# A late operand load moved behind the last transposed rows, and six result stores cut in two, in a fused backward kernel

## The chip, the cores and the metric

The kernel runs on one core of a Trainium2 chip. The metric is the device time of one execution in microseconds (us). Before the change three runs gave 823.28, 824.08 and 824.58 us, a median of 824.08 us.

The core's engines are written as the profile writes them. PE is the matrix engine, PEld is its weight load, DVE is the vector engine, ACT the scalar engine, POOL the general-purpose engine. SP is a sequencer without arithmetic; here it issues most DMAs. ACT and POOL can issue DMAs as well.

## The reference

The reference computes a transformer block and all its gradients, in bfloat16, for 2048 tokens of width 640:

```
h   = x + attn(layernorm(x))          # linear attention, 32 heads
out = h + swiglu(layernorm(h))        # hidden width F = 1728
swiglu(u) = (silu(u @ w1) * (u @ w3)) @ w2
return out, and the gradients of x, wqkv, wo, w1, w3, w2 for a given grad_out
```

The last part of the kernel matters here: the gradients of w1 and w3, each 640 x 1728. They are hn^T @ gg, where hn (2048 x 640) is the normalised input of the MLP and gg (2048 x 3456) holds the gradients behind w1 and w3 side by side. Just before it stands the gradient of x: per 128 tokens, [g_q, g_k, pk] (128 x 1920) times the transposed wqkv.

## The kernel before

The kernel is one hand-ordered program: each engine gets its instructions in the order of the Python code, and waits on semaphores where data must be there first. Two stages concern us.

**The gradient of x** (loop at L1515) runs over t = 0 to 15, 128 tokens each. `e_gxn(t)` (L1495) makes 30 matmuls on PE: two column halves of 320, each of 15 terms. Terms 0 to 4 read the transposed g_q of these tokens, terms 5 to 9 the transposed g_k, terms 10 to 14 `pkT`. The two transposes are DMAs made by `e_T` (L1489 to L1493) and issued by SP three steps ahead: `e_T(t + 3)` stands behind `e_gxn(t)`. They land in one of three buffers in turn, two of them inside `bd`, one named `gT`. After the matmuls, ACT and DVE finish the layer norm's gradient (L1139 to L1152), and SP stores the row (L1522). Every third step also has a small matmul job for another gradient, whose result SP stores at L1337.

**The gradients of w1 and w3** (loop at L1538) run over seven blocks of 496 columns of gg (480 in the last), and in each over m = 0 to 4, 128 rows of the result. One job (`grad_halves`, L1325) is 16 matmuls at L1331 that contract over the tokens. ACT copies the result out of PSUM (L1335) and issues the store (L1337). Eight PSUM buffers are at hand for the jobs (`njob = 8`). The very last job is cut into 352 and 128 columns. A block's operand `gb`, [token, column], is brought in by a transposing DMA from DRAM (`load_block`, L1471 to L1477), with two buffers. Block i + 2 is loaded when block i is through.

Block 0 is loaded in three parts, of 160, 160 and 176 columns, during the stage before: behind the steps t = 7, 9 and 11 (L1525). Block 1 is loaded behind t = 13. All these DMAs are issued by SP, in the order of the code, so a load stands in one queue with the transposes of `e_T` and the stores of L1522.

**Semaphores.** DMAs issued by SP and ACT tell of their landing on eight semaphores, handed out in turn in the order of the code; here they are called 0 to 7. At the end of the program SP waits for each of the eight, 0 first and 7 last, one instruction each, and then the engines meet in a barrier. Before the change the last store of all (128 columns) has semaphore 1, and the one before it (352 columns) has semaphore 0.

```
        if t in (7, 9, 11):
            load_block(0, (t - 7) // 2 * NB0, (t - 5) // 2 * NB0 if t < 11 else NB)
        if t == 13:
            load_block(1)
...
            for a, b in ((0, n - P), (n - P, n)) if last else ((0, n),):
                grad_job(hnN, m, lambda t: gb[i][:, t, a:b], b - a, both_grads(m, f0 + a, f0 + b), A.dma_start)
        load_block(i + 2)
```

Of the kernel before, what the change touches and what calls it, by code (L numbers as in the profile page):

```python
# [20 lines left out]
ST, DT = S // P, D // P  # L21
# [5 lines left out]
NB = 496  # L27
# [28 lines left out]
def kernel(  # L56
# [19 lines left out]
    V, A, T, G, SY = nc.vector, nc.scalar, nc.tensor, nc.gpsimd, nc.sync  # L76
# [901 lines left out]
    for c in range(SC):  # L978
# [9 lines left out]
        for fc in range(FT):  # L988
# [8 lines left out]
            if c == 0 and fc in (5, 7, 9, 11):  # L997
                a, b = {5: (0, 3), 7: (3, 6), 9: (6, 10), 11: (10, 13)}[fc]
# [13 lines left out]
            if c == SC - 1 and fc in (1, 2, 5, 6):  # L1012
                i = (1, 2, 5, 6).index(fc)
# [61 lines left out]
    for fc in range(FT - 1):  # L1075
        b, i = divmod(fc, 4)
# [154 lines left out]
    xnT, pkb, gb = {}, {}, {}  # L1231
# [55 lines left out]
    a, b = ST - 1, ST - 2  # L1287
# [33 lines left out]
    def grad_job(lhs, m, rhs, n, out, q=dma):  # L1321
        for _ in grad_halves(lhs, m, rhs, n, out, q):
            pass

    def grad_halves(lhs, m, rhs, n, out, q=dma):  # L1325

        acc = ps.tile([P, 512], F32, name="job", bufs=njob)
        for t in range(ST):
            if t == ST // 2:
                yield  # L1330
            T.matmul(acc[:, 0:n], lhsT=lhs[:, t, m * P:(m + 1) * P], rhs=rhs(t), start=(t == 0),  # L1331
                     stop=(t == ST - 1))
        ob = obs[:, cnt[0] % (OB // n) * n:(cnt[0] % (OB // n) + 1) * n]
        cnt[0] += 1
        A.copy(out=ob, in_=acc[:, 0:n])  # L1335
        for x, y, to in out:
            q(out=to, in_=ob[:, x:y])  # L1337
# [35 lines left out]
    def fill(n):  # L1373
        for _ in range(n):
            next(jobs, None)
# [55 lines left out]
    for t in range(ST):  # L1431
        c, i = divmod(t, TPC)
# [34 lines left out]
    hnN = bv.tile([P, ST, D], BF16, name="hnN")  # L1467
    blocks = [(f0, min(f0 + NB, 2 * F)) for f0 in range(0, 2 * F, NB)]
    NB0 = 160

    def load_block(i, a=0, b=NB):  # L1471
        if i < len(blocks):
            f0, f1 = blocks[i]
            if a == 0:
                gb[i] = ex.tile([P, ST, NB], BF16, name="gb", bufs=2)
            b = min(b, f1 - f0)
            dmaT(out=gb[i][:, :, a:b], in_=gg_d[f0 + a:f0 + b, :])  # L1477

    def both_grads(m, f0, f1):

        return [(max(f0, lo) - f0, min(f1, lo + F) - f0, out[:, m, max(f0, lo) - lo:min(f1, lo + F) - lo])
                for lo, out in ((0, out4S), (F, out5S)) if max(f0, lo) < min(f1, lo + F)]

    def load_hnN(i):
        dma(out=hnN[:, i * TPC:(i + 1) * TPC, :], in_=hn_v[:, i * TPC:(i + 1) * TPC, :])
# [3 lines left out]
    def e_T(t, k):  # L1489
        if k == 0:  # L1490
            gT[t] = (ex.tile([P, 2 * DT, P], BF16, name="gT") if t % 3 == 2 else
                     bd[:, 2 * (t % 3):2 * (t % 3) + 2, :].rearrange("p c (k q) -> p (c k) q", q=P))
        dmaT(out=gT[t][:, k * DT:(k + 1) * DT, :], in_=gqkv[k][:, t, :])  # L1493

    def e_gxn(t):  # L1495
        acc = ps.tile([P, 2, 512], F32, name="gxn", tag="gxn", bufs=2)
        for j in range(2):
            for k in range(15):
                g = gT[t][:, k, :] if k < 2 * DT else pkT[:, k - 2 * DT, t * P:(t + 1) * P]
                T.matmul(acc[:, j, 0:HD], lhsT=g, rhs=wqT[:, k, j * HD:(j + 1) * HD], start=(k == 0),  # L1500
                         stop=(k == 14))
        gx = scr[:, t % 2, :]
        ln_bwd(acc, t, xnN[:, t, :], ln1, gx, g_h[:, t, :], ex, scr[:, 2 + t % 2, :], scr[:, 4, :])()
        return gx
# [10 lines left out]
    for t in range(ST):  # L1515
        if t > 1 and t % 3 == 0:
            fill(2)
        gx = e_gxn(t)
        if t + 3 < ST:
            for k in range(2):  # L1520
                e_T(t + 3, k)
        dma(out=out1S[:, t, :], in_=gx)  # L1522
        if t in (2, 3, 5, 6):
            load_hnN((2, 3, 5, 6).index(t))
        if t in (7, 9, 11):  # L1525
            load_block(0, (t - 7) // 2 * NB0, (t - 5) // 2 * NB0 if t < 11 else NB)
        if t == 13:
            load_block(1)
    for _ in jobs:
# [8 lines left out]
    for i, (f0, f1) in enumerate(blocks):  # L1538
        n = f1 - f0
        for m in range(DT):  # L1540
            last = (i, m) == (len(blocks) - 1, DT - 1)
            for a, b in ((0, n - P), (n - P, n)) if last else ((0, n),):
                grad_job(hnN, m, lambda t: gb[i][:, t, a:b], b - a, both_grads(m, f0 + a, f0 + b), A.dma_start)
        load_block(i + 2)
    ps.release()
    ex.release()
# [34 lines left out]
```

## Time and profile before

| | |
|---|---|
| runs, us | 823.28, 824.08, 824.58 (median 824.08) |
| the profiled execution, us | 824.66, of which the span in the profile is 822.9 |
| granted clock of PE | 1.0 over the whole span |
| busy: PE, PEld, DVE, ACT, POOL | 99%, 62%, 55%, 40%, 16% |
| stage "gradient of x", us from the span's start | 627 to 702.7 |
| stage "gradients of w1 and w3" | 702.7 to the end |

The span starts with the first instruction and ends with the last. The profile's views that are used are: the page (busy time by engine, the chain of waits that ended last), the list of waits (who waited for whom), the timeline of one engine (start, length, what), the time from issue to landing of a DMA, and the table of busy time and DMA traffic by short windows. A line number names the line of the kernel that made the instruction.

### The profile page before, as it was taken

Reading aid. Unit: us, or ns where it says so; the run is one execution under the profiler, and the core shown is the slowest. Engines: PE = TensorE matmul, PEld = TensorE weight load, DVE = VectorE, ACT = ScalarE, POOL = GpSimd, SP = SyncE. Lnnn points to the kernel's source line nnn. Section 1 sums busy time; section 2 is a strip of 40 time slices with the busy share of each in tenths; the row PEclk is TensorE's granted clock in tenths of the full one; section 3 lists DMA queues with packets and bytes.
Section 4 is the critical chain, followed back from the end, with each engine's and each line's share of the span. In section 5 each row is a group of like instructions: output and inputs, shape, how many; then the busy total and the mean of one; then the engine's idle time right before and its main releaser. Section 6 shows DMA issues by size and latency. Waiting matters only on the chain.

```text
span 822.9 us, 14052 instructions
## 1 busy us (share of the span) xinstructions
PE 814.6 (99%) x5464; PEld 513.2 (62%) x5464; DVE 453.2 (55%) x976; ACT 325.1 (40%) x605; POOL 131.1 (16%) x193
## 2 busy tenths in 40 slices
PE   8999999999999999999999999999999999999998
PEld 5677544555555555777777777777777776544444
DVE  7859887999898576300057777772771545100000
ACT  7856788655565666011112212222212433211111
POOL 2233333323222212100001111110210000000000
PEclk9999999999999999999999999999999999999999
DMA  9999989696475556999878898369997898978661
GB/s 218 260 281 230 209 234 316 194 240 156 145 214 155 171 172 167 241 251 227 241 176 184 215 185 198 58 126 179 234 206 136 169 193 162 223 157 197 166 134 37
DMA packets 321826, 157.57 MB, mean 191 GB/s; under 512 B 240096, under 2 KB 315008, under 8 KB 321760
## 3 DMA queue, kind: packets, MB, share of 16 engines
q1 hardware_dynamic: 279712, 115.85, 62.9%
q10 hardware_dynamic: 34720, 16.34, 9.3%
q0 software_dynamic: 7328, 24.48, 9.2%
q8 instruction: 43, 0.70, 0.4%
q14 instruction: 23, 0.19, 0.1%
HBM read 47.09 MB, written 51.13 MB: 119 GB/s over the span
## 4 chain that ended last, share of the span: by engine, by line
PE 96%; DMA 2%; ACT 1%; SPq 0%; DVE 0%; issue 0%; DVEq 0%; ACTq 0%
PE mm L387 20%; PE job L1331 19%; PE ghn L1127 14%; PE gxn L1500 8%; PE gw L1082 7%; PE o L895 4%; PE big L267 4%; PE o L841 3%; PE gwo L1215 3%; PE gr L1184 3%; PE dkv L1437 3%; PE macc L422 2%; PE at L648 2%; PE mm L267 1%; DMA pqT<-pql 1%; DMA x_sb<-in_A_x_dram 1%
## 5 line engine op out<-in xcount | busy, mean ns | idle before, releaser
L1331 PE MATMUL job<-gb,hnN 128*128 128x496 bf16 (+3 forms) x576 | 116.8, 366 | 0.0
L1127 PEld LDWEIGHTS <-ggb 128*128 128x128 bf16 x864 | 84.5, 98 | 32.8
L1331 PEld LDWEIGHTS <-hnN 128*128 128x128 bf16 x576 | 55.8, 98 | 61.0
L387 PE MATMUL mm<-pqT,w 128*128 128x512 bf16 x405 | 93.6, 379 | 0.0
L387 PEld LDWEIGHTS <-w 128*128 128x128 bf16 x540 | 52.5, 98 | 63.1 <-issue 0.8
L1335 ACT CAST obs<-job 128x496 bf16<-128x496 f32 (+4 forms) x56 | 28.5, 509 | 123.7 <-PE job L1331 123.7
L1127 PE MATMUL ghn<-w13a,ggb 128*128 128x320 bf16 x448 | 63.5, 299 | 0.0
L1142 DVE SCALAR_TENSOR_TENSOR wb<-gs,hnb 128x640 f32<-128x640 bf16 x16 | 13.2, 825 | 89.8 <-ACT gs L1139 89.8
L1127 PE MATMUL ghn<-w13b,ggb 128*128 128x320 bf16 x416 | 61.4, 299 | 0.0
L387 PE MATMUL mm<-g2T,w2T 128*128 128x512 bf16 x240 | 59.6, 379 | 0.0
L1082 PE MATMUL gw<-g,hb 128*128 128x320 bf16 x416 | 56.8, 299 | 0.0
L1192 POOL TENSOR_TENSOR sz<-Zb,g_h 128x640 f32<-128x640 bf16 x16 | 20.2, 1261 | 197.7 <-DVE g_h L1193 197.7
L1082 PEld LDWEIGHTS <-hb 128*128 128x128 bf16 x416 | 40.6, 98 | 16.0 <-issue 0.3
L412 ACT CAST ghh<-mm 128x512 bf16<-128x512 f32 x48 | 28.3, 589 | 45.0 <-PE mm L387 39.7
L778 ACT ACTIVATE sig<-mm 128x512 bf16<-128x512 f32 x56 | 33.7, 602 | 25.6 <-PE mm L387 22.0
L1139 ACT ACTIVATE gs<-ghn 128x640 bf16<-128x640 f32 x16 | 11.2, 703 | 78.8 <-PE ghn L1127 63.2
L387 PEld LDWEIGHTS <-w2T 128*128 128x128 bf16 x260 | 25.3, 98 | 23.5 <-DMA w2T<-in_B_w_dram 0.2
L267 PEld LDWEIGHTS <-pqT 128*128 128x128 bf16 x320 | 30.6, 98 | 14.3 <-issue 1.7
L267 PE MATMUL big<-wqkv,pqT 128*128 128x320 bf16 x250 | 38.5, 299 | 0.3
L1331 PEld LDWEIGHTS <-g 128*128 128x128 bf16 x320 | 31.0, 98 | 11.5
L814 DVE TENSOR_TENSOR gate<-gate,sig 128x1024 bf16<-128x1024 bf16 x28 | 19.3, 689 | 33.5 <-ACT gate L789 33.5
L1500 PE MATMUL gxn<-wqT,bd 128*128 128x320 bf16 x220 | 33.7, 299 | 1.5 <-DMA bd<-g_q 1.1
(216 smaller groups left out, 1373.5 us busy)
## 6 DMA issues: line engine op xcount, KB each, us to landing
hh_d<-hhT SPq DMA_DIRECT2D x24, 256.0 KB, 2.6
gg_d<-gate POOLq DMA_DIRECT2D x24, 256.0 KB, 4.5
gg_d<-ghh POOLq DMA_DIRECT2D x24, 256.0 KB, 3.7
ggb<-gg_d SPq DMA_DIRECT2D x6, 896.0 KB, 5.3
ggb<-gg_d ACTq DMA_DIRECT2D x6, 832.0 KB, 5.8
x_sb<-in_A_x_dram SPq DMA_DIRECT2D x6, 640.0 KB, 5.9
ggb<-gg_d SPq DMA_DIRECT2D x2, 1728.0 KB, 12.9
out_dram<-obs ACTq DMA_DIRECT2D x25, 124.0 KB, 3.1
```

Source lines behind the costliest of these rows:

```text
L267: T.matmul(acc, lhsT=pqT[:, c, t * P:(t + 1) * P], rhs=wqkv[:, c, n0:n0 + HD], start=(c == 0), stop=(c == DT - 1))
L387: T.matmul(acc[:], lhsT=w[:, c, fc * P:(fc + 1) * P], rhs=rhs[:, c, :], start=(c == 0), stop=(c == DT - 1))
L412: A.copy(out=ghh[n // 2][:, n % 2, :], in_=acc[:])
L778: A.activation(sig[:, i, :], gp[:], AF.Sigmoid)
L841: T.matmul(accs[i, j][:, 0:HD], lhsT=hhT[c][:, fc, i * P:(i + 1) * P], rhs=w2[:, fc, j * HD:(j + 1) * HD], start=(first and fc == 0), stop ...
L895: T.matmul(o2["ps"][:, 0:HD], lhsT=hhT[c][:, fc, i * P:(i + 1) * P], rhs=w2[:, fc, j * HD:(j + 1) * HD], start=(fc == 0), stop=(fc == FT - 1))
L1082: T.matmul(acc[:, j, 0:HD], lhsT=hb[b][:, t, i * P:(i + 1) * P], rhs=g2[:, t, j * HD:(j + 1) * HD], start=(t == 0), stop=(t == ST - 1))
L1127: T.matmul(acc[:, j, 0:HD], lhsT=ggb[t // 2][:, k, lo:lo + P], rhs=rhs[:, j * HD:(j + 1) * HD], start=(k == 0), stop=(k == NG - 1))
L1184: T.matmul(gr[t][:, j, 0:HD], lhsT=ghT[t][:, c, :], rhs=wT2[:, c, j * HD:(j + 1) * HD], start=(c == 0), stop=(c == DT - 1))
L1331: T.matmul(acc[:, 0:n], lhsT=lhs[:, t, m * P:(m + 1) * P], rhs=rhs(t), start=(t == 0), stop=(t == ST - 1))
L1335: A.copy(out=ob, in_=acc[:, 0:n])
L1500: T.matmul(acc[:, j, 0:HD], lhsT=g, rhs=wqT[:, k, j * HD:(j + 1) * HD], start=(k == 0), stop=(k == 14))
```

## The change

Two edits. The third part of block 0 (176 columns) is loaded behind step t = 12 and no longer behind t = 11. And the results of the first six jobs of the last stage are stored in two column halves each, 248 columns, where one store of 496 columns was.

```diff
-        if t in (7, 9, 11):
-            load_block(0, (t - 7) // 2 * NB0, (t - 5) // 2 * NB0 if t < 11 else NB)
+        if t in (7, 9, 12):
+            load_block(0, (t - 7) // 2 * NB0, (t - 5) // 2 * NB0 if t < 12 else NB)
...
+                c = (a + b) // 2
+                halves = ((a, c), (c, b)) if i * DT + m < 6 else ((a, b),)
+                out = [(x + y - a, z + y - a, to) for y, w in halves for x, z, to in both_grads(m, f0 + y, f0 + w)]
-                grad_job(hnN, m, lambda t: gb[i][:, t, a:b], b - a, both_grads(m, f0 + a, f0 + b), A.dma_start)
+                grad_job(hnN, m, lambda t: gb[i][:, t, a:b], b - a, out, A.dma_start)
```

The order of SP's DMAs around the first edit (the number in brackets is the step of the row):

```
before: store row (11), LOAD 176, store of a small job, transpose g_q (15), transpose g_k (15),
        store row (12), store row (13), load block 1, store rows (14), (15)
after:  store row (11), store of a small job, transpose g_q (15), transpose g_k (15),
        store row (12), LOAD 176, store row (13), load block 1, store rows (14), (15)
```

The six DMAs that the second edit adds shift the count of semaphores: the last store gets semaphore 7, the one before it semaphore 6. PE, DVE and POOL have the same instructions in the same order as before; ACT has six more DMA issues.

## Prediction

> **What bounds the kernel now.** I read the page first: which engine is busy, and the chain of work that ended last.
>
> ```profile
> PE 814.6 (99%) x5464; PEld 513.2 (62%) x5464; DVE 453.2 (55%) x976; ACT 325.1 (40%) x605; POOL 131.1 (16%) x193
> ...
> PE 96%; DMA 2%; ACT 1%; SPq 0%; DVE 0%; issue 0%; DVEq 0%; ACTq 0%
> ```
>
> PE is never short of work for long, so a change that leaves PE's instructions alone can gain only where PE waits, or behind its last matmul. Next I read the waits of PE between 690 and 703 us, where both stages meet. There are only two:
>
> ```profile
> PE gxn L1500 <- DMA bd<-g_q: 1.1, 1, 1.1
> PE gxn L1500 <- DMA bd<-g_k: 0.4, 1, 0.4
> ```
>
> These are the transposed rows of the last step, t = 15. The idle time understates the loss, since the ends of matmuls are modelled; starts do not depend on that. PE's timeline:
>
> ```profile
> 688.58 1.52 PE L1500 MATMUL gxn<-wqT,bd 128*128 128x320 bf16 x10
> ...
> 692.65 1.52 PE L1500 MATMUL gxn<-wqT,gT 128*128 128x320 bf16 x10
> ...
> 697.98 0.85 PE L1500 MATMUL gxn<-wqT,bd 128*128 128x320 bf16 x5 [1.09 <-DMA bd<-g_q]
> 699.28 0.85 PE L1500 MATMUL gxn<-wqT,bd 128*128 128x320 bf16 x5 [0.44 <-DMA bd<-g_k]
> ...
> 702.69 4.55 PE L1331 MATMUL job<-gb,hnN 128*128 128x496 bf16 x21
> ```
>
> Step 13 starts at 688.58, step 14 at 692.65: 4.07 us a step. Step 15 should then start at 696.72 and the first job of the last stage at 696.72 + 4.07 = 700.79. It starts at 702.69. **The stall costs 1.90 us.** Why the rows come late stands in SP's timeline:
>
> ```profile
> 688.96 1.83 SPq L1522 DMA_DIRECT2D out_dram<-scr  x1
> 690.85 3.77 SPq L1477 DMA_TRANSPOSE gb<-gg_d  x1
> 694.71 0.53 SPq L1337 DMA_DIRECT2D out_dram<-obs  x1
> 695.34 1.21 SPq L1493 DMA_TRANSPOSE bd<-g_q  x1
> 696.63 1.23 SPq L1493 DMA_TRANSPOSE bd<-g_k  x1
> ```
>
> The issue of the 176-column load holds SP for 3.77 us, and both transposes stand behind it. Each lands 2.6 us after its issue: 695.34 + 2.6 = 697.94 and 696.63 + 2.6 = 699.23, the very times at which PE goes on.
>
> Last, the end of the program, from the instructions of SP's closing line in narrow windows:
>
> ```profile
> L1576 SPq EVENT_SEMAPHORE  x1: 28/28/28, 820.8 to 820.8; - x1
> L1576 SPq EVENT_SEMAPHORE  x7: 28/28/28, 821.3 to 821.7; - x7
> L1576 SPq DRAIN  x2: 7/7/7, 821.8 to 821.8; - x2
> ```
>
> The first wait that matters ends at 820.8, when the store before the last has landed. The next ends at 821.3: the last store, issued at 819.82, landed 1.5 us later. Six more waits follow, for semaphores 2 to 7 whose stores landed long before. Narrower windows put the first of the seven at 821.34, the seventh at 821.71: six steps of 0.062 us.
>
> **The change, part by part.** *The transposes move ahead of the load.* In the new order the small job's store follows row 11's store, which ends at 690.79. Its issue takes 0.53 and the gaps between issues are some 0.1 us: g_q's transpose is issued at 690.79 + 0.1 + 0.53 + 0.09 = 691.51, g_k's at 691.51 + 1.21 + 0.09 = 692.81. The small job's result is ready (ACT copied it at 686.22), the buffer is free (step 12 left PE at 688.58). Landing after 2.6 us gives 694.1 and 695.4. PE wants them at 696.72 and, five matmuls of 0.136 us later, 697.4. Even at the slowest landing of a transpose in these rows (4.3 us, the g_k issued at 687.60) they come at 695.8 and 697.1. So this stall goes whole: **-1.90 us**, if nothing else is late.
>
> *What is late next: the moved load.* The first job of the last stage reads all three parts of block 0, at 700.79. Behind g_k's issue (ends 694.04) comes row 12's store (0.09 + 0.53; its data was ready at 693.09), then the load at 694.75. What the three parts took from issue to landing, from the view of each DMA's landing (issued at 668.83, 680.51 and 690.85):
>
> ```profile
> gb<-gg_d SPq DMA_TRANSPOSE x1, 7.2
> gb<-gg_d SPq DMA_TRANSPOSE x1, 4.8
> gb<-gg_d SPq DMA_TRANSPOSE x1, 5.9
> ```
>
> The load has 700.79 - 694.75 = 6.04 us. The second row is the nearest in its surroundings: it too stood behind two transposes and a row's store. For 176 columns in place of 160 that is 4.8 x 1.1 = 5.3 us. The moved load's own row, 5.9, holds a queue that had just been blocked. The first row, 7.2, stood behind a 640 KB load and is the far end. I take 5.3 to 5.9: landing at 700.0 to 700.65, in time by 0.1 to 0.8 us, cost nothing. At 7.2 it lands at 701.95 and takes back 1.16 us. Below nothing there is no room, since PE has no other wait here.
>
> *SP behind the load.* Row 13's store and block 1's load follow. The issues ahead of block 1's load are the same ones, so it stays near 699.0, lands 10.4 us later as before (709.4) and is wanted five jobs of 3.34 us after 700.79, at 717.5. The cover is 8 us. Later loads are released by PE itself and move with it.
>
> *Six more stores on ACT.* An issue takes 0.34 us and ACT idles 2.77 us before every copy: 6 x 0.34 = 2.0 us spread over six gaps. The store of the fourth job now waits for the semaphore of the 5.67 us transpose issued at 708.61 (landing 8.5 us later, 717.1), and ACT's copies queue behind it for some 2 us; eight PSUM buffers give PE over 20 us. Cost: 0. From the other side, if they delayed the loads of `gb`, a cover of 6 us on block 2 (released 717.7, landing 10.4 later, wanted at 734.2) would have to go first.
>
> On these stores the Trainium skill speaks against the change: the page "DMA: Bandwidth & Descriptors", section Specifications, asks for at least 512 B per transfer and says that smaller ones are read, modified and written; 248 columns are 496 B. The trace has such stores: those of 240 columns (60 KB) landed in a median of 2.8 us, those of 496 columns (124 KB) in 3.1 us, so half the bytes take nearly as long. By the rule or by the row the sum is the same here, since no engine waits for a landing.
>
> *The end.* The last store has semaphore 7, so the six waits behind its landing come before it, while SP is idle: 6 x 0.062 = **-0.37 us**. If the waits ran in another order it would be 0; they run 0 to 7, as the two waits ahead of the six show.
>
> **Sum:** -1.90 - 0.37 = -2.27 us. The profiled execution took 824.66 us (span 822.9 and 1.76 around it) and becomes 822.39. It lies 0.58 above the median of the runs; from the median, 824.08 - 2.27 = **821.8 us**.
>
> **Rivals.** (a) *The moved load is late.* By the row of 7.2 us the first job waits 1.16 us: gain 1.11, time 823.0. For it: only 6.04 us of cover, and one of three rows is beyond. Against: the row with the same neighbours is well inside.
>
> (b) *The stall is not there in ordinary runs.* Step 15 misses its rows by 1.22 us, and SP lost 1.3 of that in one store (1.83 us where others took 0.53). In the table by short windows the DMAs move 0 to 10 GB/s from 689.8 to 691.0, where the windows around have over 100; the DMA view of 688 to 692 us also shows an instruction load of 0.02 MB, and the two may belong together. An execution in which the DMAs don't stop there has no stall to remove: gain 0.37, time 823.7. For it: the runs differ by 1.3 us among themselves, and the profiled one is above all three. Against: the instruction load belongs to the program, not to the run.
>
> (c) *Slower.* The moved load is now the last thing before PE's next stage, where it used to have 6 us to spare (landed 696.75, read at 702.69). If a stop like that of 689.8 to 691.0 (1.2 us) falls on top of the slowest row, landing takes 7.2 + 1.2 = 8.4, at 703.15, and PE starts 0.46 later than before; less 0.37, 0.1 slower: 824.2. It decides from 8.3 us on (694.75 + 8.3 = 702.69 + 0.37), and over 0.2% it needs 10 us.
>
> **Numbers.** A measurement of this kernel tells 0.2% (1.65 us) from no change. The full gain (821.8): 0.62. (a): 0.17. (b): 0.15. (c): 0.04; others 0.02. The range runs from 821.2, 0.6 below the forecast as the runs scatter around their median, to 823.7, which takes in (a) and reaches (b). Faster by over 0.2%: most of the first case and a third of (a), 0.63. Slower by over 0.2%: 0.03. Within: 0.34.
>
> **What would show it.** Right: no wait of PE for `bd` in step 15, the first job about 8.15 us behind step 14's start (2 x 4.07), and one closing wait behind the last landing where seven were. Wrong: a wait of PE for `gb` at L1331, or a new stall at the start of block 1 or 2. Rival (b) would show as a profile without the stall whose time is nevertheless about that of before.

## The result, and the profile after

Twelve runs of the changed kernel gave a median of 822.28 us, twelve of the kernel before 824.06 us: 1.78 us less. The ratio estimated from the single runs is 0.9983, with a 95% interval of 0.9975 to 0.9992: 1.4 us less, somewhere between 0.7 and 2.1. That is faster than before, clear of the scatter. Against the 0.2% that the prediction set as its line it is just under by the ratio (0.17%) and just over by the medians (0.22%). The forecast was 821.8, with a range of 821.2 to 823.7. The profiled execution took 822.18 us, with a span of 820.4.

The list of PE's waits between 640 and 720 us, which held two lines before, is empty. PE's timeline at the same place, the starts of steps 14 and 15 and of the first job:

```profile
692.47 1.52 PE L1500 MATMUL gxn<-wqT,gT 128*128 128x320 bf16 x10
...
696.55 1.52 PE L1500 MATMUL gxn<-wqT,bd 128*128 128x320 bf16 x10
...
700.62 5.60 PE L1331 MATMUL job<-gb,hnN 128*128 128x496 bf16 x26
```

Step 15 follows step 14 after 4.08 us and the first job comes 8.15 us behind step 14, where it took 10.03 before (702.69 - 692.65 = 10.04 from the rounded rows). The two waits, each with five matmuls alone behind it, are gone. SP's timeline shows what was swapped:

```profile
688.86 1.68 SPq L1522 DMA_DIRECT2D out_dram<-scr  x1
690.63 0.39 SPq L1337 DMA_DIRECT2D out_dram<-obs  x1
691.11 1.22 SPq L1493 DMA_TRANSPOSE bd<-g_q  x1
692.42 1.22 SPq L1493 DMA_TRANSPOSE bd<-g_k  x1
693.74 0.53 SPq L1522 DMA_DIRECT2D out_dram<-scr  x1
694.32 3.17 SPq L1477 DMA_TRANSPOSE gb<-gg_d  x1
```

The two transposes are issued 4.2 us sooner than before. Their time from issue to landing is 2.6 us each, so they land at 693.7 and 695.0, and PE reads them from 696.55 on. The load now stands behind them. Its landing, from the view of that one DMA:

```profile
gb<-gg_d SPq DMA_TRANSPOSE x1, 5.2
```

694.32 + 5.2 = 699.5, 1.1 us ahead of the first job. At the end of the program SP's last wait, and then its closing drain:

```profile
L1579 SPq DRAIN  x2: 7/7/7, 819.3 to 819.4; - x2
L1579 SPq EVENT_SEMAPHORE  x1: 28/28/28, 819.2 to 819.2; - x1
```

One wait stands at 819.2 where seven stood before, and the drain follows at 819.3. From the last landing to the drain it is 0.08 us; it was 0.45.

### The profile page after: what moved, and what is told of

The parts are those of the page before. It is cut to its first block, busy times and chain, and to the rows that moved or that the text cites. A ratio compares the mean times of both kernels' runs of the same rounds, so it can differ in the third digit from the quotient of the medians.

```text
span 820.4 us, 14028 instructions
## 1 busy us (share of the span) xinstructions
PE 812.7 (99%) x5437; PEld 512.9 (63%) x5464; DVE 453.0 (55%) x976; ACT 325.3 (40%) x605; POOL 131.0 (16%) x193
## 4 chain that ended last, share of the span: by engine, by line
PE 95%; DMA 3%; DVE 1%; ACT 1%; issue 0%; SPq 0%; DVEq 0%
PE mm L387 20%; PE job L1331 20%; PE ghn L1127 14%; PE gxn L1500 8%; PE gw L1082 7%; PE o L895 4%; PE o L841 3%; PE big L267 3%; PE gwo L1215 3%; PE gr L1184 3%; PE dkv L1437 3%; PE macc L422 2%; PE at L648 2%; PE mm L267 1%; DMA pqT<-pql 1%; DMA wqkv<-in_A_wqkv_dram 1%
## 5 line engine op out<-in xcount | busy, mean ns | idle before, releaser
L789 ACT CAST gate<-mm 128x512 bf16<-128x512 f32 x56 | 33.6, 600 | 4.1 <-DMA gg_d<-gate 4.0
```

The lines of the kernel that those rows point to most:

```text
L789: A.copy(out=gate[:, i, :], in_=gp[:])
```

## The experiments

Each run was profiled; e1's profile, which took twice the time, is not in the table. The table cuts the span of each profile into stretches: the start of the x-gradient's first matmul; the start of step 14 to the first job of the last stage, minus the 8.15 us of a run without a wait (this is the stall); the matmuls of the last stage from first start to last start; last landing to SP's closing drain. The stretch from the first matmul to step 14 was 65.74 us in all of them (to 0.01), the last matmul to its landing 2.01 to 2.06, the drain to the end 1.10 to 1.13.

| profile | first matmul at | stall | last stage's matmuls | landing to drain | span |
|---|---|---|---|---|---|
| before | 626.91 | 1.88 | 116.58 | 0.45 | 822.87 |
| before, again (e4) | 626.96 | 2.09 | 116.58 | 0.45 | 823.16 |
| before, third profile (e9) | 626.14 | 1.53 | 116.58 | 0.45 | 821.77 |
| before, fourth profile (e10) | 626.60 | 0.75 | 116.58 | 0.45 | 821.45 |
| halves alone (e2) | 629.90 | 2.19 | 116.58 | 0.08 | 825.80 |
| changed | 626.73 | 0 | 116.58 | 0.08 | 820.42 |
| changed, again (e7) | 626.38 | 0 | 116.58 | 0.08 | 820.08 |
| load alone (e8) | 626.29 | 0 | 116.58 | 0.45 | 820.39 |
| seven halves (e6) | 627.68 | 0 | 116.58 | 0.51 | 821.79 |
| load behind 13 (e3) | 628.78 | 2.45 | 118.27 | 0.08 | 826.59 |
| rows stored by ACT (e5) | 626.30 | 0.51 | 116.58 | 0.45 | 820.90 |

**e1 and e8: the load alone.** The first edit without the second.

```diff
-        if t in (7, 9, 11):
-            load_block(0, (t - 7) // 2 * NB0, (t - 5) // 2 * NB0 if t < 11 else NB)
+        if t in (7, 9, 12):
+            load_block(0, (t - 7) // 2 * NB0, (t - 5) // 2 * NB0 if t < 12 else NB)
```

> Only the load is moved; the stores are whole, so the last store has semaphore 1 again. Theory A (PE's wait for the rows of step 15, caused by the load standing ahead of them in SP's queue, is most of the gain): no wait of PE for bd in step 15, first job 8.15 us behind step 14's start, seven closing waits behind the last landing, some 1.9 us less than before in the profile and 1.4 to 1.9 in the median of runs. Theory B (the runs differ among themselves by about 2 us for a reason outside this stage, and the median moved with that): median within 0.5 us of before.

One execution of twelve, the profiled one, took 1745.76 us, about twice as long over the whole span, and says nothing here. The median of the other eleven is 822.79 us against 824.3 of the kernel before beside it, 1.5 us less; the ratio is 0.9985, interval 0.9977 to 0.9994. The same kernel was profiled once more.

> The load moved alone, for a profile. Theory A: no wait of PE for bd or gb, first job 8.15 us behind step 14's start, seven closing waits over 0.37 us behind the last landing.

That execution took 822.17 us. PE's list of waits is empty, the first job comes 8.15 us behind step 14, and the closing waits of the kernel before are still there:

```profile
L1576 SPq EVENT_SEMAPHORE  x7: 28/28/28, 818.8 to 819.2; - x7
```

So the moved load alone takes the stall away, and leaves the end as it was. Theory B falls.

**e2: the halves alone.** The second edit without the first; of its lines only the one that counts the halved stores is shown.

```diff
...
+                halves = ((a, c), (c, b)) if i * DT + m < 6 else ((a, b),)
...
```

> Only the six stores are halved; the load stays behind step 11. Theory A: PE still waits some 1.9 us for the rows of step 15, and one closing wait stands behind the last landing in place of seven: 0.37 us less than before in the end of the profile, 0 to 0.7 in the median of runs. Theory B, with the stores as the cause: 1.5 us or more less than before.

Median 823.83 against 824.3 us: ratio 0.9998, interval 0.9988 to 1.0009. By time alone this can't be told from no change. The profile can tell. PE's waits, in which the stall stands as before:

```profile
PE gxn L1500 <- DMA bd<-g_q: 1.4, 1, 1.4
PE gxn L1500 <- DMA bd<-g_k: 0.5, 1, 0.5
```

Its landing to drain is 0.08 us. The halves do what the prediction said, at the end and only there.

**e6: seven halves.** One more store is cut, so that the last store gets semaphore 0, the first in SP's order of waits. The edit is shown against the changed kernel.

```diff
-                halves = ((a, c), (c, b)) if i * DT + m < 6 else ((a, b),)
+                halves = ((a, c), (c, b)) if i * DT + m < 7 else ((a, b),)
```

> As the changed kernel, but seven stores are halved in place of six, so the last store has semaphore 0 and the one before it 7. If SP's closing waits run from 0 to 7 and the steps behind the last landing are all that the halves change: eight closing waits stand behind the last landing, 7 x 0.062 = 0.43 us more than the changed kernel in the end of the profile, and about 0.4 in the median of runs, with no wait of PE. If halves had another effect (traffic, ACT's queue), one more would go on in the direction of six: same or lower time than the changed kernel's.

SP's closing waits behind the last landing at 820.18:

```profile
L1579 SPq EVENT_SEMAPHORE  x8: 28/28/28, 820.2 to 820.6; - x8
```

Eight waits, 0.51 us from landing to drain, 0.43 more than with six halves, as expected to the second digit. The medians of runs don't show it: 822.51 us here, 822.68 for the changed kernel beside it, with runs of either kernel spread over more than 1.2 us. The step is shown by the profile, not by the times.

**e3: the load one step later still,** behind row 13's store, with the halves. The edit is shown against the changed kernel.

```diff
-        if t in (7, 9, 12):
-            load_block(0, (t - 7) // 2 * NB0, (t - 5) // 2 * NB0 if t < 12 else NB)
+        if t in (7, 9, 13):
+            k = (7, 9, 13).index(t)
+            load_block(0, k * NB0, (k + 1) * NB0 if k < 2 else NB)
```

> As the changed kernel, but the third part is loaded one step later still, behind row 13's store. Theory A with the cover of 6.04 us as its limit: row 13's result is there at about 697.0, the load is issued at about 697.7 and lands 5.2 to 5.9 us later, 702.9 to 703.6, while the first job would start at 700.6: PE waits 2.3 to 3.0 us for gb at L1331, the time is 2.3 to 3.0 us above the changed kernel's, so at or above before's. Theory C (the place in the queue hardly matters once the rows of step 15 are ahead): time as the changed kernel's.

Median 825.96 against 824.3 us: ratio 1.0021, interval 1.001 to 1.0033, slower than before. The wait that theory A named is there, in PE's waits and in its timeline:

```profile
PE job L1331 <- DMA gb<-gg_d: 2.3, 1, 2.3
```

```profile
694.52 1.52 PE L1500 MATMUL gxn<-wqT,gT 128*128 128x320 bf16 x10
...
705.12 3.37 PE L1331 MATMUL job<-gb,hnN 128*128 128x496 bf16 x8 [2.29 <-DMA gb<-gg_d]
```

694.52 + 8.15 = 702.67, so the wait costs 2.45 us, inside the 2.3 to 3.0 that were expected. But the table has a second loss which nobody expected: the matmuls of the last stage take 118.27 us and not 116.58. The table by short windows shows where (the three figures at the end are the granted clock of PE, the share of DMA, GB/s):

```profile
704.00:705.00 1.00, 0.00 (x0) 0.00 (x0) 0.97 (x5) 0.00 (x0) 0.00 (x0) 1.00 0.87 196
705.00:706.00 1.00, 0.88 (x3) 0.40 (x3) 0.64 (x1) 0.27 (x1) 0.00 (x0) 0.63 1.07 180
706.00:707.00 1.00, 1.00 (x4) 0.30 (x2) 0.32 (x1) 0.65 (x1) 0.00 (x0) 0.50 1.28 289
707.00:708.00 1.00, 1.00 (x4) 0.43 (x3) 0.18 (x1) 0.00 (x0) 0.00 (x0) 0.50 1.27 289
708.00:709.00 1.00, 1.00 (x5) 0.37 (x4) 0.00 (x0) 0.00 (x0) 0.00 (x0) 0.66 1.28 291
709.00:710.00 1.00, 1.00 (x7) 0.45 (x5) 0.00 (x0) 0.00 (x0) 0.00 (x0) 1.00 1.28 290
```

PE restarts at 705.12 and from about 705.3 to 708.7 its clock is 0.50. Over 3.4 us that is 1.7 us of lost work, which is the 1.69 of the table. So in this execution a wait of 2.45 us cost 4.1. Against the changed kernel's 1.78 below before, this kernel's 1.66 above makes 3.4 us between their medians, more than the 2.3 to 3.0 of theory A and between the two amounts. The mean clock that is on record for each run points to the reason: 3.4 us at half clock lower it to 0.998. Seven of this kernel's twelve runs have 0.997 or 0.998 (median 826.6 us) and five have 0.999 or 1.0 (median 825.5 us), where one run of the changed kernel's twelve and one of the 35 of before have 0.998.

**e5: the rows of steps 8 to 15 stored by ACT,** with the load where it was before, and whole stores.

```diff
-        dma(out=out1S[:, t, :], in_=gx)
+        (A.dma_start if t > 7 else dma)(out=out1S[:, t, :], in_=gx)
```

> As the kernel before (load behind step 11, whole stores), but the rows of steps 8 to 15 are stored by ACT and no longer by SP. It asks what the transposes of step 15 are late for. Theory A1 (issue slots: SP has been issuing without a gap since 668.8, and each issue ahead of them counts): the stores of rows 8 to 11 leave 3 x 0.53 + 1.83 + 4 x 0.09 = 3.8 us on SP where 1.3 are missing, so PE doesn't wait for bd in step 15, and the time is some 1.9 us below before's. Theory A2 (bytes: the transposes wait for the load's data on the DMA engines): the bytes are the same, so the stall of 1.9 to 2.2 us stays, and the time with it.

Median 822.81 against 824.45 us: ratio 0.9978, interval 0.9969 to 0.9987. The stall shrinks to 0.51 us but is not gone, so theory A1's forecast of no wait was missed:

```profile
PE gxn L1500 <- DMA bd<-g_q: 0.3, 1, 0.3
```

One part of the reason stands in SP's timeline:

```profile
685.35 1.27 SPq L1493 DMA_TRANSPOSE gT<-g_k  x1
686.67 4.96 SPq L1477 DMA_TRANSPOSE gb<-gg_d  x1
691.73 0.53 SPq L1337 DMA_DIRECT2D out_dram<-obs  x1
692.37 1.21 SPq L1493 DMA_TRANSPOSE bd<-g_q  x1
```

The stores' slots were saved, but the load itself now takes 4.96 us to issue where it took 3.77: the stretch from 690.5 to 691.5, in which the DMAs move 5 to 10 GB/s, falls into it. Measured from step 14's start (692.04) the transposes gain 2.36 us and not 3.8. Even so g_q's rows would be in time: landing after 2.6 us, as before, they come at 694.97, and PE wants them at 692.04 + 4.07 = 696.11. The other part is their landing, which took longer:

```profile
bd<-g_q SPq DMA_TRANSPOSE x1, 4.1
```

That is 696.5, and PE goes on at 696.54. So what is left of the stall comes from a slower landing, not from SP's queue. The load, issued at 686.67 and landing after 8.6 us, was still on its way until 695.28, and ACT issued a row's store at 692.69; which of them slowed the transpose was not separated. Theory A2, by which nothing should have changed, falls for the stall of 1.9 us: there the transposes landed within 2.6 us, and the same bytes left only 0.51 of it here. That remainder can be a matter of bytes. Theory A1 holds for what stands ahead in SP's queue, but a slot is not a fixed price: an issue that falls into the stretch in which the DMAs hardly move takes longer. The median is only 0.13 us above that of e7 beside it, where the stretches of the two profiles differ by 0.88; one profile of each can't say why.

**e4, e9, e10: the kernel before again.**

> The kernel before once more. Theory A with the stall differing from run to run: a profile of about 824.3 us shows a stall of PE in step 15 near 1.9 us, a profile of about 822.2 us shows next to none. Theory B: the stall is in either, and the difference lies elsewhere in the span.

Median 824.72 against 824.3 us for the same kernel beside it, so the measurement itself wanders by 0.4 us. The profile, of an execution of 824.94 us, has a stall of 2.09 us. Two more executions were profiled, each once:

> The kernel before, one more profile. Theory A: the wait for the rows of step 15 belongs to the program; first job 9.9 to 10.4 us behind step 14's start, and what differs between runs stands ahead of the stage (its first matmul at 626 to 630 us). Rival (b) of the prediction: some executions have no such wait (8.15 us).

They took 823.56 and 823.23 us (a single run of the kernel before beside them: 825.24) and had stalls of 1.53 and 0.75 us. Theory A allowed 9.9 to 10.4 us behind step 14's start, so stalls of 1.75 to 2.25; both are smaller, and neither is gone. The SP timeline of the second, to be held beside that of before in the prediction:

```profile
688.28 0.53 SPq L1522 DMA_DIRECT2D out_dram<-scr  x1
688.86 4.32 SPq L1477 DMA_TRANSPOSE gb<-gg_d  x1
693.28 0.53 SPq L1337 DMA_DIRECT2D out_dram<-obs  x1
```

Row 11's store takes 0.53 here, the other three profiles of this kernel have 1.6 to 1.8; the load takes 4.32 where they have 3.4 to 3.9. The small job's store comes at 693.28 instead of 694.71; measured from step 14's start (692.35 here, 692.65 there) it is 1.13 us sooner, which is the whole difference between the stalls of 0.75 and 1.88. Of this, 0.75 us lie in the two issues, and 0.38 in SP's having reached them sooner. So the stall belongs to the program, since every profile with the load at its old place has one, but its size to the run.

**e7: the changed kernel again,** beside e5 and e6.

> The changed kernel once more, beside the other kernels of this call. Theory A: no wait of PE between 640 and 720 us, one closing wait behind the last landing, 1.5 to 2.3 us below before. Against it: a wait of PE for gb at the first job in its profile, or a median within 1 us of before's.

Median 822.68 against 824.45 us: ratio 0.9981, interval 0.9972 to 0.999. By the medians that is 1.77 us, as at first; by the ratio 1.6. There is no wait of PE.

## Why the prediction was right, point by point

*The transposes move ahead of the load: -1.90 us.* Right, and in the profile to 0.02: the stall is 1.88 there and 0 after. The transposes landed 0.4 us sooner than worked out: row 11's store ended 0.25 us sooner, and the small job's store took 0.39 and not 0.53. e8 shows that the moved load does this alone.

*The moved load is in time.* Right. It was issued at 694.32 (worked out: 694.75), took 5.2 us (taken: 5.3 to 5.9) and had 1.1 us to spare. The row chosen as nearest, that of the second part, was the right one for this profile; in e6, e7 and e8 the load took 5.6 to 5.7 us, inside what was taken, and had 0.65 to 1.2 us to spare. e3 shows that this cover was a real limit: one step further, and the load is what PE waits for.

*SP behind the load, six more stores on ACT: 0.* Right. The last stage's matmuls take 116.58 us in the profile before and after. Block 1's load was issued at 698.16 (before: 699.01). The fourth job's stores were held back by some 0.2 us, not 2, since the transposing DMA ahead of them also came sooner. The halved stores of 62 KB landed in a median of 3.6 us, the whole ones of 124 KB at the same place before in 3.2; so half the bytes took no less time, much as the row of 240 columns had it in the prediction, and nothing waited for them.

*The end: -0.37 us.* Right: 0.45 to 0.08 in the profile, alone in e2, and turned round to 0.51 in e6.

*The sum: 2.27 us.* Right for the profiled execution: 1.88 + 0.37 = 2.25 of its 2.45 us of span; 0.18 of the rest lie ahead of the stage, where the first matmul came at 626.73 and not at 626.91. Too large for the runs: 1.78 by the medians, and 1.77 in e7; 1.4 and 1.6 by the ratios. The interval of the first comparison ends at 2.1, that of e7 at 2.3. The mis-sized term is the stall. The prediction took it from one execution and carried it over to the median whole. In the five profiles with the load at its old place (e5, with the stores moved, left aside) it is 1.88, 2.09, 1.53, 0.75 and 2.19, a mean of 1.69; with 0.37 for the end that makes 2.06. What is left between 2.06 and 1.78 can't be told from the scatter.

*Rival (a)* and *rival (c)* did not come about. What they would have cost was counted by the wait alone. For (a), 1.16 us, no run speaks against that. The wait of (c) would have been 703.15 - 700.79 = 2.36 us, and in e3 a wait of that size was followed by another 1.69 us at the low clock: (c) was priced too low. *Rival (b)* was right in kind, not in size: an ordinary run can have much less of the stall (0.75 us), and the argument against it, that the stop of the DMAs belongs to the program, also holds, since all four profiles of this kernel have one (4 to 10 GB/s for 0.7 to 1.2 us). In e10 it found SP in the load and not in row 11's store.

*What stays open.* An instruction load lies about 1 us ahead of the stop of the DMAs in the profiles of before and after. Whether it causes the stop was not tried. The Trainium skill, on the page "Runtime: NRT & Kernel Launch", section Instruction fetch mechanics, calls the cost of such a load mostly hidden. For PE that agrees, it goes on matmul by matmul; for SP's queue 1.3 us of one store's issue stand beside it here.

## What to carry to other kernels

When an engine that is busy 99% of the time waits once, look at what the late DMA's issuer was doing just before: a long transposing load can hold its queue for 3 to 5 us, and what is wanted sooner has to stand ahead of it. Take the loss from starts of matmuls, not from idle time, check the cover of what is moved back against its own nearest landing, and read a stall in several executions before it is promised to the median. A step of a few tenths of a us at the end of a program can be read exactly in the profile even where the times of runs can't show it.

## What was not expected of the hardware

A wait of PE can cost more than its length. In e3 PE stood idle for 2.29 us and then worked at a clock of 0.50 for 3.4 us, which cost 1.69 us more; the waits of 1.09 and 0.44 us in the kernel before, and one of 1.40 us in e2, left the clock at 1.00. In e2's profile a stretch of the same kind lies at 99.6 to 103.0 us. Ahead of it stands the only other idle time of PE over 2 us in the profiles of the table:

```profile
98.36 0.81 PE L750 MATMUL trh<-ident,hn 128*128 128x128 bf16 x10 [2.27 <-DVE hn L160]
```

```profile
99.60:103.00 3.40, 3.40 (x10) 1.21 (x8) 3.23 (x9) 1.20 (x3) 0.12 (x1) 0.50 1.03 261
```

Its first matmul of the x-gradient comes at 629.90, where eight others have 626.1 to 627.0. So part of the scatter of runs comes from there; another part doesn't, since e6 and e3 have 627.68 and 628.78 without such a stretch ahead of it. No run sets the length of a wait on purpose, so where between 1.40 and 2.27 us the limit lies, and whether the length alone decides, stays open.

The Trainium skill, on the page "TensorE: Matmul & The Clock Gate", section HAM oscillation — how this bites in real kernels, warns of idle gaps of more than about 3.4 us. In e3 2.29 us were enough and in e2 2.27; here the measurement decides.
